# Two weight matrices kept in DRAM unsplit, one load fewer at the start, attention in pairs: a change to an attention-and-two-MLP kernel

## Chip, core and metric

The kernel runs on one core of a Trainium2 chip. The metric is the device time of one execution in microseconds (us), as a median over executions; lower is better.

## What is computed

Eight heads of attention over 4 batches of 576 tokens, four heads with a local mask (a window of 32 keys) and four with a strided one (every 32nd key); then two multilayer blocks over the 2304 tokens:

```
attn = softmax(mask(q k^T / 8)) v              # B=4, H=8, S=576, D=64
x    = attn as (2304, 512)
x    = (((x @ w1) * (x @ w2)) @ w3) @ w_out     # 512 -> 1024 -> 1024 -> 512
h    = x @ w_in                                 # 512 -> 2048
out  = (h * sigmoid(1.702 h)) @ w_out2          # 2048 -> 512
```

The weights arrive as 8-byte floats.

## The kernel before

Every matmul operand is held as two parts, hi and lo, whose sum is the fp32 value, and every product is three matmuls (hi·lo, lo·hi, hi·hi). Making the two parts is a **split**: `split_hi` (L171) is a copy on ACT, `split_lo` (L177) a subtraction on DVE. A weight piece of 8-byte floats (1 MB, 128 x 1024 values) is turned to fp32 by `to_f32`: L192 and L193 on ACT, L194, L195 and L196 on DVE.

The program runs in these stages (times from the profiled execution):

- **Start, 0 to 36 us.** Attention of batch 0, in 11 parts (`a_load`, `a_scores`, `a_trans`, `a_pv`), beside the first pieces of w1 and w2 (`c_load` fetches, `c_do` converts).
- **First layer of batches 0 and 1, 36 to 198 us.** `g1` (matmuls L354) makes (x w1)(x w2). The attention of the next batches and the conversion of the other pieces are woven in. Half of the results go to DRAM (`abdram`) and come back later.
- **Fold, 198 to 236 us.** `w_group` (L468) multiplies w3 by w_out once, so that the first block's second half is one product.
- **Back region, 236 to 316 us.** `g2` (matmuls L400, copy `ysb` L406, write to `ydram` L408) for batches 0 and 1; the results parked in `abdram` are read back and split (`back`, L389, tile `ab`). Attention parts of batch 2, and units 0 to 3 of w_in, are woven in.
- **Batch 2, 316 to 405 us, and batch 3, 405 to 487 us.** `g1` and `g2` of these; the other units of w_in in batch 2; the eight units of the second w_out (units 8 to 15) in batch 3.
- **Second block, 487 us to the end.** For each of 3 token blocks of 768 and each of 8 units: `quad` (7 products of 6 matmuls, L657, by a Strassen-like scheme, adds L663, gelu L648) and `o_group` (L703).

A **unit** is handled by `u_load` (fetch, L526) and `u_conv`. A w_in unit is converted into tile `x`, four sums or differences are added to it, the seven 256-wide factors are split into tile `hl` (128 x 1792 twice) and written to `widram` (L544). A w_out unit is converted into `x`, split back into its own `raw` tile and written to `wodram` (L551). In the second block `w_load` reads `hl` straight from `widram` (L614) and `wt_load` reads a w_out unit straight into its slot (L637); all eight `wt_load` are issued ahead of the first quad. `x` is one buffer; `raw` is two.

The order of instructions on each engine is fixed before the run by a scheduler, from the order in which `weave` emits the steps of several lists; each engine runs its list in order. All DMAs are issued by SP, in its order, on one queue.

Of the kernel before, what the change touches and what calls it, by code (L numbers as in the profile page):

```python
# [11 lines left out]
F32 = mybir.dt.float32  # L12
F32R = mybir.dt.float32r
# [3 lines left out]
I64 = mybir.dt.int64  # L17
# [4 lines left out]
P = 128  # L22
B, H, S, D = 4, 8, 576, 64
# [4 lines left out]
STRIDE = 32  # L28
# [109 lines left out]
def body(ctx: ExitStack, tc, qk, vv, mask, w1, w2, w3t, wo, win, wout, out):  # L138
# [21 lines left out]

    ydram = dram.tile([KC, P, NT], F32, name="ydram")
    abdram = dram.tile([3, MC, P, HB], F32, name="abdram")
    widram = dram.tile([NU, P, 2, 7 * 256], F32, name="widram")
    wodram = dram.tile([NU, P, 2, CW2], F32, name="wodram")

    def r(ap):
        return ap.bitcast(F32)

    def split_hi(hi, src, eng="act"):
        if eng == "act":  # L170
            nc.scalar.activation(hi, src, AF.Copy)  # L171
# [52 lines left out]
    def a_load(n):  # L224
        if n >= n_all or n in raws:
            return
        tl = ALL[n]
        nk, w = tl.nk, 2 * (tl.nq + tl.nk)
        t = at.tile([P, ATW], F32, tag="qk", name="qk", bufs=3)
        nc.sync.dma_start(t[:, :w], qk[n, :, :w])  # L230
        u = at.tile([P, HL * D], F32, tag="v", name="v", bufs=4)
        nc.sync.dma_start(u[:nk], vv[n, :nk])
        raws[n] = (t, u)

    def a_scores(n):
        tl = ALL[n]
        nq, nk = tl.nq, tl.nk
        t, u = raws.pop(n)
        L = live[n] = dict(v=u)
        mi = MASKS.index(tl.mask)  # L240
        qs = t[:, :2 * nq].rearrange("p (h n) -> p h n", h=2)
        ks = t[:, 2 * nq:2 * (nq + nk)].rearrange("p (h n) -> p h n", h=2)
        sm = at.tile([P, HL, P], F32, tag="sm", name="sm", bufs=3)
        st = at.tile([P, 3, HL], F32, tag="st", name="st", bufs=3)

        sc = aps.tile([P, 2, 4 * P], F32, tag="sc", name="sc")
        for i in range(2):
            for g in range(2):
                rows = slice(g * D, (g + 1) * D)
                nc.tensor.matmul(  # L250
                    sc[:nq, g, i * P:i * P + nk], qs[rows, i], ks[rows, i], start=True, stop=True,
                )

        for h in range(HL):
            nc.vector.tensor_tensor_reduce(  # L255
                sm[:nq, h, :nk], sc[:nq, h // 2, h % 2 * P:h % 2 * P + nk], msk[:nq, mi, :nk], -SCALE, 3e38,
                op0=ALU.add, op1=ALU.min, accum_out=st[:nq, 0, h:h + 1],
            )
        for h in range(HL):
            nc.scalar.activation(  # L260
                sm[:nq, h, :nk], sm[:nq, h, :nk], AF.Exp, bias=st[:nq, 0, h:h + 1], scale=-1.0,
                accum_out=st[:nq, 1, h:h + 1],
            )
        nc.vector.tensor_scalar_add(st[:nq, 2], st[:nq, 1], EPS)
        nc.vector.reciprocal(st[:nq, 2], st[:nq, 2])
        nc.vector.tensor_tensor(
            sm[:nq, :, :nk], sm[:nq, :, :nk], st[:nq, 2].unsqueeze(2).to_broadcast([nq, HL, nk]), op=ALU.mult
        )
        L["sm"] = sm

# [20 lines left out]
    def a_pv(n):
        tl = ALL[n]
        nq, nk = tl.nq, tl.nk
        L = live.pop(n)
        ps = L["ps"]
        pv = aps.tile([P, 2, P], F32, tag="pv", name="pv")
        xh, xl = xt[tl.b]
        if tl.local:
            dh, dl = (x[:, 0:2, tl.o:tl.o + nq] for x in (xh, xl))
        else:  # L300
            dh, dl = (
                x[:, 2:4].rearrange("p c (j r) -> p c j r", r=STRIDE)[:, :, tl.j0:tl.j0 + tl.nj, tl.o:tl.o + tl.g]
                for x in (xh, xl)
            )

        for h in range(HL):
            rows = slice(h % 2 * D, (h % 2 + 1) * D)
            nc.tensor.matmul(  # L308
                pv[rows, h // 2, :nq], L["v"][:nk, h * D:(h + 1) * D], ps[:nk, h * nq:(h + 1) * nq],
                start=True, stop=True,  # L310
            )
        src = pv[:, :, :nq]
        if not tl.local:
            src = src.rearrange("p c (j r) -> p c j r", j=tl.nj)
        split_hi(dh, src)
        split_lo(dl, src, dh)

    def steps_for(b):

        out = []  # L320
        per = len(PARTS[b])
        for j in range(per):
            n = START[b] + j
            out.append((j + AT[0], lambda n=n: a_scores(n)))
            out.append((j + AT[1], lambda n=n: a_load(n + 2)))
            out.append((j + AT[2], lambda n=n: a_trans(n)))
            out.append((j + AT[3], lambda n=n: a_pv(n)))
        return sorted(((at / (per + AT[3] - 1), f) for at, f in out), key=lambda t: t[0])
# [120 lines left out]
    def c_load(i):  # L449
        if i < len(line):  # L450
            fetched[i] = fetch(line[i][1])

    def c_do(i):
        convert(line[i][0], fetched.pop(i))
        c_load(i + 3 if i + 3 < 20 else i + 2)

    def conv(*which):
        return [lambda i=i: c_do(i) for i in which]
# [26 lines left out]
    a_load(0)  # L485
    nc.sync.dma_start(msk, mask)
    a_load(1)
    for i in range(3):
        c_load(i)
    weave(steps_for(0), list(zip((0.1, 0.5), conv(0, 1))))  # L490

# [2 lines left out]
    def pairs(b, aways):  # L494
        return [f for m in range(MC) for hb in range(2) for f in g1(b, hb, m, hold, aways[hb])]

    places = (0.02, 0.1, 0.22, 0.34, 0.46, 0.58)
    weave(pairs(0, (None, 0)), steps_for(1), list(zip(places, conv(2, 3, 4, 5, 6, 7))))
    later = share(steps_for(2), 0.3, 0.25, 0.2, 0.25)
# [21 lines left out]
    def u_load(i):  # L521

        if i >= 2 * NU:
            return
        raw = cv[i % len(cv)].tile([P, CW2], I64, tag="raw", name="raw", bufs=2 if len(cv) == 1 else 1)
        nc.sync.dma_start(raw, win[i] if i < NU else wout[i - NU])  # L526
        todo[i] = raw

    def u_conv(i, last=False):
        raw = todo.pop(i)  # L530
        x = cv[0].tile([P, 2 * CW2], F32, tag="x", name="x")
        if i < NU:
            hl = cv[0].tile([P, 2, 7 * 256], F32R, tag="hl", name="hl")
            to_f32(x[:, :CW2], raw, CW2)
            if not last:
                u_load(i + 2)
            a21, a11, a12, a22, s1, s2, s3, s4 = (x[:, n * 256:(n + 1) * 256] for n in range(8))
            nc.vector.tensor_tensor(s1, a21, a22, op=ALU.add)
            nc.vector.tensor_tensor(s2, s1, a11, op=ALU.subtract)
            nc.vector.tensor_tensor(s3, a11, a21, op=ALU.subtract)  # L540
            nc.vector.tensor_tensor(s4, a12, s2, op=ALU.subtract)
            split_hi(hl[:, 0], x[:, 256:])
            split_lo(hl[:, 1], x[:, 256:], hl[:, 0])
            nc.sync.dma_start(widram[i], r(hl))  # L544
        else:

            to_f32(x[:, :CW2], raw, CW2)
            hl = raw.bitcast(F32R).rearrange("p (a n) -> p a n", a=2)
            split_hi(hl[:, 0], x[:, :CW2])
            split_lo(hl[:, 1], x[:, :CW2], hl[:, 0])  # L550
            nc.sync.dma_start(wodram[i - NU], r(hl))  # L551
            if not last:
                u_load(i + 2)

    def u_convs(lo, hi, ahead=True):
        return [lambda i=i: u_conv(i, not ahead and i + 2 >= hi) for i in range(lo, hi)]
# [54 lines left out]
    def w_load(n):  # L611
        if n < NB * NU:
            t = (p2 if n % 2 else cv_a).tile([P, 2, 7 * 256], F32R, tag="hl", name="hl")
            nc.sync.dma_start(r(t), widram[n % NU])  # L614
            wq[n] = t

    g = batch_groups(3)
# [16 lines left out]
    acc_l, acc_r = {}, {}  # L634

    def wt_load(i):
        nc.sync.dma_start(r(wt[i].rearrange("p a c n -> p a (c n)")), wodram[i])  # L637

    def g_split(src):
        t = ring[used[0] % len(ring)]  # L640
# [77 lines left out]

    wt_load(0)
    w_load(1)  # L720
    for i in range(1, NU):
        wt_load(i)
    for b in range(NB):
        left = [accp.tile([P, 512], F32, tag="acc", name="acc") for _ in range(HT // P)]
        for i in range(NU):
            quad(b, i, (lambda i=i: o_group(left, gl.pop(i - 1), i - 1, 0)) if i else (lambda: None))
            if i:
                o_group(left, gl.pop(NU + i - 1), i - 1, 1)
        for h in range(2):
# [45 lines left out]
```

## Time and profile before

| | |
|---|---|
| time, median of 3 (lowest to highest) | 873.87 us (873.4 to 874.31) |
| profiled execution: time, span of the core | 876.68 us, 874.9 us |
| mean granted TensorE clock | 0.982 |
| busy: PE, DVE, ACT | 830.2, 560.3, 418.3 us |
| moved by DMA | 151.77 MB |

The page of a profile has the busy time of each engine, and a chain of work that ended last. The trace behind it can be asked for the busy time of each engine in a stretch, for the waits of an engine and what ended each, and for single instructions with their start and duration. PE is TensorE, PEld its weight load, DVE VectorE, ACT ScalarE, SP the engine that issues the DMAs. A clock of 1.00 is full speed (2.4 GHz), 0.50 half.

### The profile page before, as it was taken

Reading aid. Unit: us, or ns where it says so; the run is one execution under the profiler, and the core shown is the slowest. Engines: PE = TensorE matmul, PEld = TensorE weight load, DVE = VectorE, ACT = ScalarE, POOL = GpSimd, SP = SyncE. Lnnn points to the kernel's source line nnn. Section 1 sums busy time; section 2 is a strip of 40 time slices with the busy share of each in tenths; the row PEclk is TensorE's granted clock in tenths of the full one; section 3 lists DMA queues with packets and bytes.
Section 4 is the critical chain, followed back from the end, with each engine's and each line's share of the span. In section 5 each row is a group of like instructions: output and inputs, shape, how many; then the busy total and the mean of one; then the engine's idle time right before and its main releaser. Section 6 shows DMA issues by size and latency. Waiting matters only on the chain.

```text
span 874.9 us, 13887 instructions
## 1 busy us (share of the span) xinstructions
PE 830.2 (95%) x5200; PEld 753.2 (86%) x5200; DVE 560.3 (64%) x1352; ACT 418.3 (48%) x980; POOL 1.4 (0%) x8
## 2 busy tenths in 40 slices
PE   3889999999998899999999599999999999999998
PEld 2679999987787899999999489998999988999986
DVE  6889983358888778755666356666455655655640
ACT  7888872246666556554455323344223433322330
POOL 0000000000000000000000000000000000000000
PEclk9999999999998899999999699999999999999999
DMA  8565561134477875415479964452344451344201
GB/s 294 175 228 177 165 200 58 63 120 134 139 281 254 283 272 235 159 35 203 175 273 349 349 267 169 169 190 88 112 176 152 148 194 37 136 161 161 85 36 37
DMA packets 41699, 151.77 MB, mean 173 GB/s; under 512 B 4512, under 2 KB 25888, under 8 KB 31904
## 3 DMA queue, kind: packets, MB, share of 16 engines
q1 hardware_dynamic: 41632, 150.88, 48.0%
q8 instruction: 41, 0.67, 0.3%
q14 instruction: 26, 0.21, 0.1%
HBM read 114.82 MB, written 36.04 MB: 172 GB/s over the span
## 4 chain that ended last, share of the span: by engine, by line
PE 84%; DVE 6%; ACT 5%; DMA 3%; issue 1%; SPq 0%; ACTq 0%; DVEq 0%
PE ps L354 23%; PE acc L703 23%; PE ps L657 20%; PE ps L400 10%; PE pv L308 2%; PE acc L468 2%; PE sc L250 2%; PE pt L286 1%; ACT sm L260 1%; DMA raw<-in_w3t 1%; DMA wodram<-raw 1%; DMA raw<-in_w 1%; DMA ydram<-ysb 1%; DVE xw L195 1%; DVE w L177 1%
## 5 line engine op out<-in xcount | busy, mean ns | idle before, releaser
L703 PE MATMUL acc<-w,w 128*128 128x512 f32 x864 | 204.4, 391 | 0.4 <-DVE w L177 0.4
L657 PE MATMUL ps<-yq,hl 128*128 128x384 f32 x1008 | 186.6, 341 | 10.5 <-ACT c L675 10.3
L657 PEld LDWEIGHTS ps<-yq,hl 128*128 128x128 f32 x1008 | 180.1, 190 | 14.6 <-ACT c L675 10.6
L703 PEld LDWEIGHTS acc<-w,w 128*128 128x128 f32 x864 | 161.6, 188 | 32.6 <-DVE w L177 1.2
L400 PE MATMUL ps<-ab,w 128*128 128x288 f32 x768 | 113.2, 309 | 5.8 <-DVE ab L177 2.9
L400 PEld LDWEIGHTS ps<-ab,w 128*128 128x128 f32 x768 | 109.1, 200 | 8.2 <-DVE ab L177 3.6
L354 PE MATMUL ps<-xbh,w 128*128 128x288 f32 x512 | 106.0, 300 | 0.0
L354 PE MATMUL ps<-xah,w 128*128 128x288 f32 x512 | 102.0, 295 | 0.0
L354 PEld LDWEIGHTS ps<-xbh,w 128*128 128x128 f32 x512 | 83.9, 191 | 0.8 <-issue 0.7
L354 PEld LDWEIGHTS ps<-xah,w 128*128 128x128 f32 x512 | 82.0, 188 | 0.0
L648 ACT ACTIVATE sg<-c 128x384 f32<-128x384 f32 x48 | 25.2, 525 | 115.0 <-DVE c L663 115.0
L354 PE MATMUL ps<-xbl,w 128*128 128x288 f32 x256 | 80.1, 313 | 0.0
L354 PE MATMUL ps<-xal,w 128*128 128x288 f32 x256 | 76.3, 298 | 0.0
L260 ACT ACTIVATE sm<-sm,st 96x128 f32<-96x128 f32 (+2 forms) x176 | 67.6, 387 | 13.9 <-DVE st L255 13.7
L663 DVE TENSOR_TENSOR u<-ps,u 128x384 f32<-128x384 f32 x96 | 53.3, 555 | 20.6 <-PE ps L657 19.8
L379 DVE TENSOR_TENSOR abf<-ps,abf 128x288 f32<-128x288 f32 x64 | 29.0, 453 | 40.7 <-PE ps L354 36.8
L354 PEld LDWEIGHTS ps<-xbl,w 128*128 128x128 f32 x256 | 49.1, 192 | 3.0 <-issue 0.2
L177 DVE TENSOR_TENSOR w<-gr,w 128x384 fp32r<-128x384 f32 x48 | 26.6, 558 | 38.4 <-ACT w L171 38.4
L255 DVE CUSTOM_DVE_ANT_0 sm<-sc,msk 96x128 f32<-96x128 f32 (+2 forms) x176 | 41.2, 276 | 14.2 <-PE sc L250 8.5
L468 PE MATMUL acc<-w,w 128*128 128x512 f32 x192 | 48.1, 402 | 1.2 <-ACT raw L476 0.8
L354 PEld LDWEIGHTS ps<-xal,w 128*128 128x128 f32 x256 | 48.1, 188 | 0.9 <-issue 0.2
L377 ACT ACTIVATE abf<-ps 128x288 f32<-128x288 f32 x64 | 25.8, 404 | 44.5 <-PE ps L354 44.3
(81 smaller groups left out, 1012.1 us busy)
## 6 DMA issues: line engine op xcount, KB each, us to landing
hl<-widram SPq DMA_DIRECT2D x24, 1792.0 KB
widram<-hl SPq DMA_DIRECT2D x8, 1792.0 KB
raw<-in_w3t SPq DMA_DIRECT2D x17, 512.0 KB
raw<-in_w SPq DMA_DIRECT2D x8, 1024.0 KB
raw<-in_win SPq DMA_DIRECT2D x8, 1024.0 KB
raw<-in_wout SPq DMA_DIRECT2D x8, 1024.0 KB
wodram<-raw SPq DMA_DIRECT2D x8, 1024.0 KB
w<-wodram SPq DMA_DIRECT2D x8, 1024.0 KB
```

What stands on the lines that cost most here:

```text
L177: e.tensor_tensor(lo, src, r(hi), op=ALU.subtract)
L255: nc.vector.tensor_tensor_reduce(sm[:nq, h, :nk], sc[:nq, h // 2, h % 2 * P:h % 2 * P + nk], msk[:nq, mi, :nk], -SCALE, 3e38, op0=ALU.add, ...
L260: nc.scalar.activation(sm[:nq, h, :nk], sm[:nq, h, :nk], AF.Exp, bias=st[:nq, 0, h:h + 1], scale=-1.0, accum_out=st[:nq, 1, h:h + 1],)
L354: nc.tensor.matmul(ps, ws[a][m // 2][:, at:at + P], xh[c][:, k, cols], start=(k == 0 and (a, c) == ORDER[0]), stop=(k == KC - 1 and (a, c) ...
L377: nc.scalar.activation(f, ps, AF.Copy)
L379: nc.vector.tensor_tensor(f, ps, f, op=ALU.mult)
L400: nc.tensor.matmul(st[0], wfs[a][k][:, n * P:(n + 1) * P], hold[hb, k][:, c], start=(k == 0 and (a, c) == ORDER[0]), stop=(k == MC - 1 and ...
L468: nc.tensor.matmul(acc[f], hl[:, a, f * P:(f + 1) * P], wor[c][g], start=(g == 0 and (a, c) == ORDER[0]), stop=(g == MC - 1 and (a, c) == ...
L648: nc.scalar.activation(sg, src, AF.Sigmoid, scale=1.702)
L657: nc.tensor.matmul(ps, w[:, a, f * 256 + kk * P:f * 256 + (kk + 1) * P], yq[:, b, kk, c], start=(kk == 0 and (a, c) == ORDER[0]), stop=(kk ...
L663: nc.vector.tensor_tensor(dst, x, y, op=ALU.add)
L703: nc.tensor.matmul(acc[t], g[:, a, t * P:(t + 1) * P], wt[i][:, c, half], start=(i == half == 0 and (a, c) == ORDER[0]), stop=(i == NU - 1 ...
```

## The change

Three edits:

- **Weights unsplit in DRAM.** `widram` and `wodram` hold one fp32 value where they held a hi and a lo. `u_conv` splits nothing any more and writes `x` itself (after: L562 and L564); so `x` is held until its write has landed. `w_load` reads 896 KB into `x` and splits it into `hl`, 24 times; `wt_load` reads 512 KB into `raw` and splits it into the slot, 8 times, and is issued one unit ahead of its use, not all eight at first. `u_conv` now fetches the unit after next ahead of its own write for w_out too.
- **Start.** Two weight pieces are fetched at first, not three; pieces 2 to 4 are fetched after the attention of batch 0 has been emitted.
- **Pairs.** For batches 1 to 3 two attention parts share one `a_scores` (one PSUM tile `sc`), and one `a_pv`; `qk` has 4 buffers, not 3.

```
-    widram = dram.tile([NU, P, 2, 7 * 256], F32, name="widram")
-    wodram = dram.tile([NU, P, 2, CW2], F32, name="wodram")
+    widram = dram.tile([NU, P, 7 * 256], F32, name="widram")
+    wodram = dram.tile([NU, P, CW2], F32, name="wodram")
...
+        if b:
+            for j in range(0, per, 2):
+                n = START[b] + j
+                ns = [n, n + 1][:per - j]
+                out.append((j + AT[0], lambda ns=ns: a_scores(*ns)))
+                out.append((j + 1.0, lambda n=n: a_load(n + 2)))
+                out.append((j + 1.4, lambda n=n: a_load(n + 3)))
+                out.append((j + 1.8, lambda ns=ns: [a_trans(n) for n in ns]))
+                out.append((j + 2.6, lambda ns=ns: a_pv(*ns)))
...
-        c_load(i + 3 if i + 3 < 20 else i + 2)
+        if i > 1:
+            c_load(i + 3 if i + 3 < 20 else i + 2)
...
-    for i in range(3):
+    for i in range(2):
         c_load(i)
...
+    for i in range(2, 5):
+        c_load(i)
...
         x = cv[0].tile([P, 2 * CW2], F32, tag="x", name="x")
+        to_f32(x[:, :CW2], raw, CW2)
+        if not last:
+            u_load(i + 2)
         if i < NU:
-            hl = cv[0].tile([P, 2, 7 * 256], F32R, tag="hl", name="hl")
-            to_f32(x[:, :CW2], raw, CW2)
-            if not last:
-                u_load(i + 2)
...
-            split_hi(hl[:, 0], x[:, 256:])
-            split_lo(hl[:, 1], x[:, 256:], hl[:, 0])
-            nc.sync.dma_start(widram[i], r(hl))
+            nc.sync.dma_start(widram[i], x[:, 256:])
         else:
-            to_f32(x[:, :CW2], raw, CW2)
-            hl = raw.bitcast(F32R).rearrange("p (a n) -> p a n", a=2)
-            split_hi(hl[:, 0], x[:, :CW2])
-            split_lo(hl[:, 1], x[:, :CW2], hl[:, 0])
-            nc.sync.dma_start(wodram[i - NU], r(hl))
-            if not last:
-                u_load(i + 2)
+            nc.sync.dma_start(wodram[i - NU], x[:, :CW2])
...
             t = (p2 if n % 2 else cv_a).tile([P, 2, 7 * 256], F32R, tag="hl", name="hl")
-            nc.sync.dma_start(r(t), widram[n % NU])
+            x = cv_a.tile([P, 2 * CW2], F32, tag="x", name="x")[:, 256:]
+            nc.sync.dma_start(x, widram[n % NU])
+            split_hi(t[:, 0], x)
+            split_lo(t[:, 1], x, t[:, 0])
...
     def wt_load(i):
-        nc.sync.dma_start(r(wt[i].rearrange("p a c n -> p a (c n)")), wodram[i])
+        t = cv_a.tile([P, CW2], I64, tag="raw", name="raw").bitcast(F32)[:, :CW2]
+        nc.sync.dma_start(t, wodram[i])
+        w = wt[i].rearrange("p a c n -> p a (c n)")
+        split_hi(w[:, 0], t)
+        split_lo(w[:, 1], t, w[:, 0])
...
-    for i in range(1, NU):
-        wt_load(i)
     for b in range(NB):
...
+            if b == 0 and i + 1 < NU:
+                wt_load(i + 1)
```

What this moves on the engines shows best in three places. The first is ACT at the start of the back region, before: the conversions of units 0 to 2 (`raw`, `x`), the split `hl` of unit 0, copies `ysb` and splits `ab`.

```order
L406 ACTIVATE ysb_2704<-ps_2654 128x288
L192 ACTIVATE x_2801<-raw_2646 128x1024
L193 ACTIVATE raw_2646<-raw_2646 128x1024
L406 ACTIVATE ysb_2742<-ps_2713 128x288
L193 ACTIVATE raw_2648<-raw_2648 128x1024
L171 ACTIVATE hl_2802<-x_2801 128x1792
L406 ACTIVATE ysb_2770<-ps_2745 128x288
L171 ACTIVATE ab_2819<-abf_2817 128x288
L171 ACTIVATE ab_2824<-abf_2822 128x288
L171 ACTIVATE ab_2829<-abf_2827 128x288
L406 ACTIVATE ysb_2798<-ps_2773 128x288
L193 ACTIVATE raw_2808<-raw_2808 128x1024
```

The same place after:

```order
L192 ACTIVATE x_2791<-raw_2654 128x1024
L193 ACTIVATE raw_2654<-raw_2654 128x1024
L424 ACTIVATE ysb_2691<-ps_2662 128x288
L193 ACTIVATE raw_2656<-raw_2656 128x1024
L424 ACTIVATE ysb_2732<-ps_2707 128x288
L424 ACTIVATE ysb_2760<-ps_2735 128x288
L171 ACTIVATE ab_2806<-abf_2804 128x288
L193 ACTIVATE raw_2797<-raw_2797 128x1024
L171 ACTIVATE ab_2811<-abf_2809 128x288
L171 ACTIVATE ab_2816<-abf_2814 128x288
L424 ACTIVATE ysb_2788<-ps_2763 128x288
L192 ACTIVATE x_3463<-raw_2656 128x1024
```

The 128 x 1792 split is gone from between the `ysb` copies, and the first conversion step of unit 2 (L193 on `raw_2797`), which waits for that unit's load, has moved from behind the last `ysb` of the group to between two splits of `ab`.

The second place is ACT at the end of batch 3, before: the last four `ysb` of the batch, units 14 (`x_5224`) and 15 (`x_5312`) of the weights, and the first copy `c` of the second block.

```order
L406 ACTIVATE ysb_5408<-ps_5383 128x288
L192 ACTIVATE x_5224<-raw_5089 128x1024
L193 ACTIVATE raw_5089<-raw_5089 128x1024
L406 ACTIVATE ysb_5436<-ps_5411 128x288
L171 ACTIVATE raw_5089<-x_5224 128x1024
L406 ACTIVATE ysb_5464<-ps_5439 128x288
L192 ACTIVATE x_5312<-raw_5160 128x1024
L193 ACTIVATE raw_5160<-raw_5160 128x1024
L406 ACTIVATE ysb_5492<-ps_5467 128x288
L171 ACTIVATE raw_5160<-x_5312 128x1024
L675 ACTIVATE c_5521<-ps_5514 128x384
```

After, the same four `ysb`; units 13, 14 and 15 are `x_5090`, `x_5161` and `x_5247`, with the raw tiles `raw_4962`, `raw_5027` and `raw_5096`:

```order
L424 ACTIVATE ysb_5341<-ps_5316 128x288
L424 ACTIVATE ysb_5369<-ps_5344 128x288
L424 ACTIVATE ysb_5397<-ps_5372 128x288
L193 ACTIVATE raw_5027<-raw_5027 128x1024
L192 ACTIVATE x_5090<-raw_4962 128x1024
L424 ACTIVATE ysb_5425<-ps_5400 128x288
L193 ACTIVATE raw_5096<-raw_5096 128x1024
L192 ACTIVATE x_5161<-raw_5027 128x1024
L192 ACTIVATE x_5247<-raw_5096 128x1024
L171 ACTIVATE w0_66<-raw_5434 128x1024
L693 ACTIVATE c_5457<-ps_5450 128x384
```

Unit 13 stands where unit 15 stood; units 14 and 15 and the split of the first w_out unit stand between the last `ysb` and `c`. L193 of a unit now stands ahead of L192 of the unit before it.

The third place is SP after, from the load of unit 15 (`raw_5096`) on:

```order
L547 DMA raw_5096<-in_wout 128x1024
L564 DMA wodram_87<-x_5090 128x1024
L564 DMA wodram_87<-x_5161 128x1024
L652 DMA raw_5434<-wodram_87 128x1024
L652 DMA raw_5446<-wodram_87 128x1024
L564 DMA wodram_87<-x_5247 128x1024
L626 DMA x_5439<-widram_86 128x1792
L652 DMA raw_5535<-wodram_87 128x1024
```

Before, the last write of a w_out unit was followed by direct reads into slots and `hl`; now the read of the second w_in unit (`x_5439`) needs the buffer `x` that the last write frees.

## Rows read from the trace of the kernel before

**Rows 1.** Page, busy time of PE, and shares of the chain that ended last.

```profile
PE 830.2 (95%) x5200; PEld 753.2 (86%) x5200; DVE 560.3 (64%) x1352; ACT 418.3 (48%) x980; POOL 1.4 (0%) x8
...
PE 84%; DVE 6%; ACT 5%; DMA 3%; issue 1%; SPq 0%; ACTq 0%; DVEq 0%
```

**Rows 2.** Stretches: from:to, length; busy PE, PEld, DVE, ACT, POOL; clock; DMA share; GB/s.

```profile
0.00:22.00 22.00, 8.63 (x56) 6.18 (x56) 13.49 (x42) 15.46 (x37) 1.42 (x8) 1.00 0.82 294
...
88.00:110.00 22.00, 21.98 (x190) 19.88 (x191) 21.17 (x60) 18.30 (x54) 0.00 (x0) 1.00 0.50 155
...
532.00:554.00 22.00, 22.00 (x116) 20.53 (x116) 12.86 (x26) 6.84 (x14) 0.00 (x0) 1.00 0.45 171
```

**Rows 3.** Chain of waits, start: start, us, what; then PE's waits, 0 to 66.

```profile
3.09 7.31 DMA raw<-in_w
...
PE sc L250 <- DMA qk<-in_qk: 6.1, 2, 3.2
```

**Rows 4.** The same stretches view, back region.

```profile
250.00:264.00 14.00, 11.83 (x91) 10.54 (x91) 12.82 (x43) 8.37 (x27) 0.00 (x0) 0.89 0.79 271
264.00:280.00 16.00, 12.50 (x97) 11.21 (x97) 13.20 (x38) 11.54 (x26) 0.00 (x0) 0.93 0.73 274
280.00:300.00 20.00, 19.53 (x145) 18.90 (x145) 13.93 (x39) 9.40 (x23) 0.00 (x0) 0.88 0.79 270
300.00:316.00 16.00, 13.85 (x89) 13.12 (x86) 13.32 (x43) 10.87 (x37) 0.00 (x0) 0.79 0.72 256
```

**Rows 5.** PE's waits, 198 to 310: total, times, longest.

```profile
PE ps L400 <- ACT ysb L406: 2.9, 1, 2.9
PE ps L400 <- DVE ab L177: 2.4, 2, 2.1
PE sc L250 <- DVE st L255: 2.1, 2, 1.9
```

**Rows 6.** Chain of waits, back region, three of 99 pieces.

```profile
278.28 0.40 ACT ysb L406
...
298.34 1.70 ACT hl L171
...
302.01 0.46 DVE ab L177
```

**Rows 7.** Groups by line and form: count, busy, mean ns of one, idle before.

```profile
L193 ACT ACTIVATE raw<-raw 128x1024 int32<-128x1024 uint32 x28 | 32.3, 1152 | 2.5 <-DMA raw<-in_win 1.8 <-DMA raw<-in_wo 0.7
...
L177 DVE TENSOR_TENSOR hl<-x,hl 128x1792 fp32r<-128x1792 f32 x8 | 16.2, 2024 | 5.9 <-ACT hl L171 5.9
...
L171 ACT ACTIVATE hl<-x 128x1792 fp32r<-128x1792 f32 x8 | 13.6, 1699 | 5.0 <-DVE x L541 5.0
...
L177 DVE TENSOR_TENSOR raw<-x,raw 128x1024 fp32r<-128x1024 f32 x8 | 9.8, 1223 | 5.8 <-ACT raw L171 4.7 <-DMA ydram<-ysb 1.1
```

**Rows 8.** SP and ACT, single instructions: a load, units 8, 14 and 15.

```profile
415.74 0.33 SPq L526 DMA_DIRECT2D raw<-in_wout  x1
...
420.71 1.14 ACT L192 ACTIVATE x<-raw 128x1024 f32<-128x1024 f32 x1 [0.29 <-DMA raw<-in_wout]
...
473.49 1.13 ACT L192 ACTIVATE x<-raw 128x1024 f32<-128x1024 f32 x1
...
482.54 1.13 ACT L192 ACTIVATE x<-raw 128x1024 f32<-128x1024 f32 x1 [2.65 <-DMA raw<-in_wout]
```

**Rows 9.** Chain of waits, end of batch 3, four of 33 pieces.

```profile
476.75 1.22 DVE x L196
...
485.97 2.18 DMA ydram<-ysb
...
489.39 7.54 DMA wodram<-raw
...
497.58 6.00 PE ps L657 x18
```

**Rows 10.** PE, single runs: the second quad's start.

```profile
506.87 5.46 PE L657 MATMUL ps<-yq,hl 128*128 128x384 f32 x30
```

More of the change, by code (lines that the diff above doesn't have):

```diff
@@ L228, in a_load @@
         nk, w = tl.nk, 2 * (tl.nq + tl.nk)
-        t = at.tile([P, ATW], F32, tag="qk", name="qk", bufs=3)
+        t = at.tile([P, ATW], F32, tag="qk", name="qk", bufs=4)
         nc.sync.dma_start(t[:, :w], qk[n, :, :w])
@@ L233, in a_load, with a_scores, a_soft @@
         raws[n] = (t, u)
-    def a_scores(n):
+    def a_scores(*ns):
+        sc = aps.tile([P, 2, 4 * P], F32, tag="sc", name="sc")
+        for at_c, n in zip((0, 2 * P), ns):
+            nq, nk = ALL[n].nq, ALL[n].nk
+            t, u = raws.pop(n)
+            live[n] = dict(v=u)
+            qs = t[:, :2 * nq].rearrange("p (h n) -> p h n", h=2)
+            ks = t[:, 2 * nq:2 * (nq + nk)].rearrange("p (h n) -> p h n", h=2)
+            for i in range(2):
+                for g in range(2):
+                    rows = slice(g * D, (g + 1) * D)
+                    c0 = at_c + i * P
+                    nc.tensor.matmul(sc[:nq, g, c0:c0 + nk], qs[rows, i], ks[rows, i], start=True, stop=True)
+        for at_c, n in zip((0, 2 * P), ns):
+            a_soft(n, sc[:, :, at_c:at_c + 2 * P])
+    def a_soft(n, sc):
         tl = ALL[n]
         nq, nk = tl.nq, tl.nk
-        t, u = raws.pop(n)
-        L = live[n] = dict(v=u)
+        L = live[n]
         mi = MASKS.index(tl.mask)
-        qs = t[:, :2 * nq].rearrange("p (h n) -> p h n", h=2)
-        ks = t[:, 2 * nq:2 * (nq + nk)].rearrange("p (h n) -> p h n", h=2)
         sm = at.tile([P, HL, P], F32, tag="sm", name="sm", bufs=3)
         st = at.tile([P, 3, HL], F32, tag="st", name="st", bufs=3)
[L246 to L252, printed above, removed]
         for h in range(HL):
@@ L289, in a_trans, with a_pv @@
         L["ps"] = ps
[L291 to L316, printed above, removed]
+    def a_pv(*ns):
+        pvs = aps.tile([P, 4, P], F32, tag="pv", name="pv")
+        for j, n in enumerate(ns):
+            nq, nk = ALL[n].nq, ALL[n].nk
+            L = live.pop(n)
+            ps = L["ps"]
+            for h in range(HL):
+                rows = slice(h % 2 * D, (h % 2 + 1) * D)
+                nc.tensor.matmul(
+                    pvs[rows, 2 * j + h // 2, :nq], L["v"][:nk, h * D:(h + 1) * D], ps[:nk, h * nq:(h + 1) * nq],
+                    start=True, stop=True,
+                )
+        for j, n in enumerate(ns):
+            tl = ALL[n]
+            xh, xl = xt[tl.b]
+            src = pvs[:, 2 * j:2 * j + 2, :tl.nq]
+            if tl.local:
+                dh, dl = (x[:, 0:2, tl.o:tl.o + tl.nq] for x in (xh, xl))
+            else:
+                dh, dl = (
+                    x[:, 2:4].rearrange("p c (j r) -> p c j r", r=STRIDE)[
+                        :, :, tl.j0:tl.j0 + tl.nj, tl.o:tl.o + tl.g
+                    ] for x in (xh, xl)
+                )
+                src = src.rearrange("p c (j r) -> p c j r", j=tl.nj)
+            split_hi(dh, src)
+            split_lo(dl, src, dh)
     def steps_for(b):
@@ L321, in steps_for @@
         per = len(PARTS[b])
+        if b:
[7 more added lines that the diff above has]
+                out.append((j + 2.6, lambda ns=ns: a_pv(*ns)))
+            return sorted(((at / (per + 1.7), f) for at, f in out), key=lambda t: t[0])
         for j in range(per):
@@ L487, in body @@
     a_load(1)
-    for i in range(3):
+    for i in range(2):
         c_load(i)
```

## The prediction, made before the changed kernel ran

> **What bounds the kernel now.** I read the page first: TensorE (PE) is busy for 830.2 of 874.9 us and holds 84% of the chain that ended last [rows 1]. A change that leaves the matmuls as they are, as this one does, can only move PE's idle time, 45 us, and the time at half clock behind it. So the second view is the table of stretches, to see where that idle time lies [rows 2]. In 0 to 22 us PE works for 8.63 us. In the first layer it is full, with DVE at 21.17 of 22 us, so DVE has no slack there. In the second block it is full with DVE at 12.86 and ACT at 6.84 of 22 us, so both have room. Two other holes are left: the back region [rows 4] and the boundary between batch 3 and the second block [rows 9]. The waits and the chain of these two, read third, carry the forecast.
>
> **Start and pairs: about -1 us.** Three pieces of 1 MB are queued at 3.09 us; the first lands 7.31 us later [rows 3]. The attention loads that follow stand behind all three, and PE waits 6.1 us for `qk` in two waits. With two pieces one such transfer leaves the way of those loads. But ACT is busy for 15.46 us of the first 22 [rows 2], so part of the wait comes back as a wait for ACT or DVE. I take a third of it, -2 us; bounds -5 (nearly the whole wait goes) and +1 (the third piece is now late). The conversion deferred falls into a stretch where PE is full and DVE nearly so: +1 (0 to +2). The pairs change no arithmetic. They halve the handshakes on `sc` and `pv` and make each part's result later. No row here shows a paired part; the nearest is the wait `sc` <- `st`, 2.1 us [rows 5], which halved gives -1 and doubled +2; I count it inside the back region's range.
>
> **Back region: about -9 us.** From 250 to 316 us PE is idle for 2.17 + 3.50 + 0.47 + 2.15 = 8.3 us, and the clock costs (1 - 0.89) x 14 + (1 - 0.93) x 16 + (1 - 0.88) x 20 + (1 - 0.79) x 16 = 8.4 us more [rows 4]: 16.7 us lost. What ends the waits are `ysb` on ACT and `ab` on DVE [rows 5]. Both stand behind the split of `hl` [rows 6]: one `ysb` starts at 278.28, behind a 1.70 us copy; the copy at 298.34 and its 2.02 us subtraction [rows 7] end just ahead of the `ab` at 302.01 on which PE starts again. The change takes four pairs of these out of the region (4 x 1.70 on ACT, 4 x 2.02 on DVE) and halves four writes of 1.79 MB, behind which the reads of `abdram` wait. If all of it went, the gain would be 16.7 us. But something is late next: in the new order L193 of unit 2 stands between two `ab` splits, and waits for a load of 1 MB that lands 4.97 us after its issue (415.74 to 420.71) [rows 8]. I allow 2.8 us of idle time for this (the load less what of it lies beside queued matmuls) and 1.6 us for the attention waits, which are 2.1 us now [rows 5], 4.4 in all, and as much clock loss for each idle microsecond as now (8.4 / 8.3): 16.7 - 8.8 = 8, and 1 us for the shorter writes: -9. Bounds -13 (the new wait is hidden too) and -3 (another wait of the same size in each place of the old).
>
> **Batch 2: +0.5 us.** L192 of each unit now waits until the write of `x` has landed. The eight w_in units share 236 to 405 us, some 20 us each, against a write of about 5 us (the line of the next part), so the write is over; bounds 0 and +1.5.
>
> **Boundary: about +13 us.** Before, unit 8 starts L192 at 420.71 and unit 15 at 482.54 [rows 8]: 8.83 us a unit. The last write, 7.54 us from 489.39, releases `c` and with it PE at 497.58 [rows 9]; the second quad starts at 506.87 [rows 10]. After, `x` is held until its write has landed, and on ACT, which runs its list in order, L193 of unit i+2 stands ahead of L192 of unit i+1, so that this waits for the load of unit i+2. The loop of one unit is then: L192 start to L196 end, 473.49 to 477.97 = 4.5 us [rows 8, 9]; the raw buffer is free, load of unit i+2, 5.0 us; L193, 1.15 us [rows 7]: 10.6 us, and with some of ACT's other work in it 11.2. Unit 8 itself starts later, at about 427, since the first `w_load` is now split ahead of it (1.7 + 2.0 us, behind a transfer and the batch's own copies).
>
> - Unit 14 starts at 427 + 6 x 11.2 = 494.2 and is done at 498.7.
> - Its write, 512 KB, lies between the 144 KB write of 2.18 us [rows 9] and the 1 MB load of 4.97 us: on the line between them 3.3 us. Unit 15 waits for it: 502.0.
> - Unit 15 takes 4.5 us and, with the first w_out split between its steps (1.2 us), is done at 507.7. PE starts again at about 508, not 497.58.
> - The second quad needs its `w_load`: write of unit 15, 3.3 us; read of 896 KB, by the same line 4.6 us; the split 1.7 + 2.0 us, and 0.5 us of issue: 519.8, against 506.87: +13.
>
> What PE does in the meantime, the first quad and its `o_group`, is done in both cases. Bounds: the pace of the unit is the uncertain factor; at 10.4 us a unit +8, at 11.9 us +17. [...]
>
> **Second block: +0.5 us.** 24 splits of 1.70 us on ACT and 2.02 us on DVE, and 8 smaller ones, are added. A quad with its share of `o_group` takes some 15 us of PE; DVE goes from 58% to about 72%, ACT from 31% to about 42%. PE waits for neither now, so four PSUM buffers hide it. The single `x` lets one read and split of about 8.3 us (4.6 + 1.7 + 2.0) stand in each such period. Bounds 0 and +3.
>
> **Sum.** -2 + 1 - 9 + 0.5 + 13 + 0.5 = +4 us, on the profiled execution's 876.68 us. The median is 2.8 us below that, so 873.87 + 4 = 878 us.
>
> **Rivals.**
>
> - *The boundary's chain doesn't run out (faster).* If the loads are prefetched early enough the units keep the pace of 8.83 us. Then unit 15 starts at 427 + 61.8 = 488.8, is done at 494.5, PE starts at 495, and the second quad at 494.5 + 3.3 + 4.6 + 4.2 = 506.6: no loss, and the sum is -9: 865 us. For it: of the units shown only the last waits long for its load, 2.65 us [rows 8], and the bytes are halved. Against it: the one buffer and the order on ACT. It decides whether unit 13 starts L192 before 475 us (471 by this, 483 by mine).
> - *The back region keeps its holes (slower, by more).* The splits go, but `ab` and `ysb` wait behind L193 or L192, which wait for loads. For it: queue share 0.72 to 0.79 there [rows 4]. Against it: the rows name the split, not a load. The term is -3, the sum +10: 884 us.
> - *The splits in the second block reach PE.* If the split's DVE half comes late in each period and the next `w_load` with it, a wait of 0.8 us for each of 23 quads gives +18: 892 us or more. Against it: the room in rows 2.
>
> **How the numbers follow.** About 0.2%, 1.75 us, is what a measurement of this kernel can tell from no change. Mine has 0.47 (its own range 872 to 884: slower 0.30, same 0.13, faster 0.04), the boundary without loss 0.24 (faster 0.22, same 0.02), the kept holes 0.19 (slower 0.18, same 0.01), the splits on PE 0.06 (slower), and 0.04 for what I did not think of, spread evenly. That is faster 0.28, same 0.17, slower 0.55. The range takes in the middle of the first rival and most of the second: 864 to 887.
>
> **What would show it.** In the profile after: L171 and L177 of 128 x 1792 only in the second block; PE idle and clock loss from 250 to 316 us about half of now; L192 of w_out units 11 us apart, waiting for the DMA of `wodram`; the second quad about 13 us later after the start of batch 3; DVE near 72% in the second block with PE full. It would be wrong if the last `ysb` of batch 3 were delayed so that PE stops earlier still, or if unit 15 were done before PE is.

## The result, and the profile after

The changed kernel takes 881.46 us (median of 4, 879.37 to 882.67) against 873.63 us; the ratio is 1.0091, 95% interval 1.0073 to 1.0108. It is slower by 7.8 us, where +4 was forecast. A second set of runs gave 1.0074 (1.0050 to 1.0098).

PE does the same matmuls, is busy less and idle longer, as the first rows of the page say (against [rows 1]; 877.6 - 818.5 = 59 us idle, 45 before):

```profile
PE 818.5 (93%) x5200; PEld 746.2 (85%) x5200; DVE 585.1 (67%) x1368; ACT 437.4 (50%) x996; POOL 1.4 (0%) x8
...
PE 67%; DMA 12%; ACT 9%; DVE 9%; issue 2%; SPq 1%; ACTq 0%; DVEq 0%
```

DMA's share of the chain has gone from 3% to 12%, though 114 MB are moved where 152 MB were. To see where the time went, each stage is taken from the first matmul of its kind to the first of the next stage (first layer, fold, `g2`, batch 2, batch 3, first quad, second quad); by this measure the fold begins at 183 us before. In us, with one profiled execution of each kernel; "start", "pairs" and "unsplit" are one edit alone, and they and the last two columns are the experiments below:

| stage | before | after | after, 2nd | start | pairs | unsplit | two x | start + pairs |
|---|---|---|---|---|---|---|---|---|
| start | 35.8 | 31.9 | 31.7 | 30.3 | 35.2 | 34.6 | 31.5 | 31.6 |
| first layer | 147.3 | 145.1 | 145.5 | 148.6 | 147.1 | 148.7 | 145.9 | 145.9 |
| fold | 53.0 | 53.8 | 53.4 | 53.7 | 53.4 | 53.5 | 53.7 | 52.9 |
| back region | 79.0 | 63.2 | 63.5 | 78.6 | 69.0 | 61.6 | 62.4 | 70.3 |
| batch 2 | 90.3 | 97.0 | 97.4 | 90.3 | 86.9 | 98.3 | 91.4 | 86.9 |
| batch 3 | 77.0 | 83.1 | 85.8 | 77.0 | 77.7 | 78.8 | 85.7 | 77.0 |
| to the second quad | 24.5 | 33.1 | 33.3 | 21.5 | 21.2 | 41.2 | 11.7 | 19.3 |
| rest | 368.0 | 370.3 | 370.1 | 368.1 | 368.0 | 370.3 | 371.5 | 368.0 |
| span | 874.9 | 877.6 | 880.8 | 868.1 | 858.6 | 886.9 | 853.8 | 852.0 |

So the changed kernel won 15.8 us in the back region and 5.3 us before it (3.9 and 2.2, less 0.8 in the fold), and gave 6.7 us back in batch 2, 6.1 in batch 3, 8.7 at the boundary and 2.3 in the second block. In these two executions that is +2.7 us, where the medians say +7.8.

A stage also gets shorter when work leaves it. The back region and batch 2, before and after, as whole stretches:

```profile
236.06:315.08 79.02, 70.74 (x520) 66.26 (x518) 61.60 (x180) 49.00 (x129) 0.00 (x0) 0.89 0.76 270
315.08:405.42 90.34, 90.34 (x729) 85.36 (x727) 62.00 (x177) 45.92 (x121) 0.00 (x0) 1.00 0.49 183
230.79:293.96 63.17, 58.99 (x468) 55.74 (x466) 38.68 (x105) 32.37 (x80) 0.00 (x0) 1.00 0.69 234
293.96:391.00 97.04, 92.06 (x757) 88.61 (x757) 66.65 (x234) 47.37 (x156) 0.00 (x0) 0.96 0.35 125
```

After the change 52 matmuls fewer fall into the back region (468, not 520) and 28 more into batch 2: attention parts that the new order puts elsewhere. Of the 15.8 us, PE's idle time is 4.1 (8.3 before, 4.2 after) and its busy time 11.7; the busy part holds both the clock and the moved matmuls, which are worth some 3 us by an estimate from the trace (sixteen `sc` took 1.06 us at full clock).

The stretches of the after kernel (columns as in [rows 2]), which answer to [rows 2, 4]; the rows from 231 to 294 us are its back region:

```profile
0.00:22.00 22.00, 11.61 (x76) 8.16 (x76) 13.47 (x53) 14.87 (x43) 1.42 (x8) 1.00 0.82 281
231.00:245.00 14.00, 13.80 (x105) 13.57 (x104) 7.27 (x13) 7.50 (x12) 0.00 (x0) 1.00 0.64 238
245.00:259.00 14.00, 12.52 (x104) 11.32 (x103) 11.02 (x41) 7.52 (x26) 0.00 (x0) 1.00 0.70 217
259.00:273.00 14.00, 12.06 (x102) 11.20 (x101) 8.66 (x26) 8.25 (x23) 0.00 (x0) 1.00 0.67 219
273.00:294.00 21.00, 20.43 (x163) 19.49 (x161) 11.52 (x27) 9.03 (x18) 0.00 (x0) 1.00 0.72 251
308.00:330.00 22.00, 20.12 (x175) 18.95 (x173) 15.13 (x61) 12.05 (x40) 0.00 (x0) 1.00 0.64 229
330.00:352.00 22.00, 18.91 (x146) 18.34 (x147) 16.58 (x53) 10.27 (x37) 0.00 (x0) 0.84 0.27 95
462.00:484.00 22.00, 15.85 (x99) 15.53 (x99) 6.10 (x7) 4.79 (x7) 0.00 (x0) 0.84 0.54 170
484.00:506.00 22.00, 7.15 (x27) 6.25 (x28) 15.07 (x21) 9.75 (x13) 0.00 (x0) 0.62 0.46 160
```

In the back region PE is idle for 4.2 us and the clock stays at 1.00 throughout. In batch 2 (328 to 333 us) and between 458 and 498 us there are new holes, and each has a clock below 1.00 in the row in which it ends. In the second block PE is full, with DVE at 230 of 344 us (189 before):

```profile
532.00:876.00 344.00, 339.14 (x1684) 305.29 (x1683) 188.72 (x353) 113.54 (x218) 0.00 (x0) 1.00 0.34 126
532.00:876.00 344.00, 341.63 (x1694) 306.58 (x1692) 229.67 (x377) 143.41 (x241) 0.00 (x0) 1.00 0.23 79
```

The first row is before, the second after. PE's waits (total, times, longest), the first line before, the others after, against [rows 3, 5]:

```profile
PE ps L657 <- ACT c L675: 10.3, 1, 10.3
PE ps L675 <- ACT c L693: 19.0, 1, 19.0
PE ps L418 <- DVE ab L177: 13.6, 6, 5.0
PE sc L249 <- DMA qk<-in_qk: 3.3, 1, 3.3
PE sc L249 <- DVE st L262: 2.3, 3, 1.5
```

The chain of waits in batch 2 shows where one of the `ab` waits, 5.0 us, comes from:

```profile
321.68 5.43 DMA raw<-in_win
...
327.13 1.13 ACT raw L193
328.26 1.54 ACT sm L267 x8
...
332.69 0.36 DVE ab L177
...
333.09 7.18 PE ps L418 x39
```

ACT stood at L193 of a w_in unit until its load had landed (3.0 us of idle time); the exponentials of an attention part and the split `ab` were behind it in ACT's list, and PE behind these.

At the boundary, L192 and L193 of the w_out units on ACT (in brackets the idle time before and what ended it), which answer to [rows 8]; then the chain of waits, against [rows 9], and PE:

```profile
410.72 1.14 ACT L192 ACTIVATE x<-raw 128x1024 f32<-128x1024 f32 x1 [1.46 <-DVE hl L177]
...
446.42 1.12 ACT L193 ACTIVATE raw<-raw 128x1024 int32<-128x1024 uint32 x1 [4.67 <-DMA raw<-in_wout]
...
482.85 1.10 ACT L193 ACTIVATE raw<-raw 128x1024 int32<-128x1024 uint32 x1 [8.04 <-DMA raw<-in_wout]
484.05 1.12 ACT L192 ACTIVATE x<-raw 128x1024 f32<-128x1024 f32 x1
491.39 1.12 ACT L192 ACTIVATE x<-raw 128x1024 f32<-128x1024 f32 x1 [6.23 <-DMA wodram<-x]
```

```profile
440.30 6.09 DMA raw<-in_wout
...
453.36 7.00 DMA wodram<-x
...
477.35 6.67 DMA wodram<-x
...
484.05 1.13 ACT x L192
...
487.19 1.24 DVE x L196
...
488.44 2.87 DMA wodram<-x
...
491.39 1.12 ACT x L192
```

```profile
497.47 4.97 PE L675 MATMUL ps<-yq,hl 128*128 128x384 f32 x18 [18.97 <-ACT c L693]
503.82 3.63 PE L721 MATMUL acc<-w,w 128*128 128x512 f32 x14 [1.38 <-ACT w L171]
507.29 0.87 PE L675 MATMUL ps<-yq,hl 128*128 128x384 f32 x4
```

Unit 14 starts at 484.05, 73.3 us after unit 8: 12.2 us a unit, where it was 8.83. Unit 15 waits for the write of unit 14, and `c` for unit 15; PE stands for 19 us. SP issues the load of a later unit just ahead of the write that frees `x`:

```profile
452.98 0.33 SPq L547 DMA_DIRECT2D raw<-in_wout  x1
453.36 0.42 SPq L564 DMA_DIRECT2D wodram<-x  x1
```

That write landed after 7.00 us and the one at 477.35, also behind a load, after 6.67; the last one, with no load ahead of it, after 2.87. So a conversion of 4.4 us (484.05 to 488.43) and a write of some 7 us behind a load make up most of the 12.2 us; the load itself takes 6.09 us in the chain.

### The profile page after: what moved, and what is told of

Same layout as the page of the kernel before. It is cut to its first block, busy times and chain, and to the rows that moved or that the text cites. A ratio compares the mean times of both kernels' runs of the same rounds, so it can differ in the third digit from the quotient of the medians.

```text
span 877.6 us, 13922 instructions
## 1 busy us (share of the span) xinstructions
PE 818.5 (93%) x5200; PEld 746.2 (85%) x5200; DVE 585.1 (67%) x1368; ACT 437.4 (50%) x996; POOL 1.4 (0%) x8
## 4 chain that ended last, share of the span: by engine, by line
PE 67%; DMA 12%; ACT 9%; DVE 9%; issue 2%; SPq 1%; ACTq 0%; DVEq 0%
PE acc L721 22%; PE ps L675 19%; PE ps L372 13%; PE ps L418 7%; DMA wodram<-x 4%; ACT sm L267 2%; PE sc L249 2%; DMA widram<-x 2%; PE pv L306 2%; DMA raw<-in_w3t 1%; ACT xw L192 1%; ACT x L192 1%; PE pt L293 1%; DMA ydram<-ysb 1%; DVE w L177 1%
## 5 line engine op out<-in xcount | busy, mean ns | idle before, releaser
L675 PE MATMUL ps<-yq,hl 128*128 128x384 f32 x1008 | 185.9, 339 | 20.2 <-ACT c L693 19.0
L675 PEld LDWEIGHTS ps<-yq,hl 128*128 128x128 f32 x1008 | 179.2, 189 | 24.6 <-ACT c L693 19.3
L418 PE MATMUL ps<-ab,w 128*128 128x288 f32 x768 | 109.8, 302 | 13.6 <-DVE ab L177 13.6
L418 PEld LDWEIGHTS ps<-ab,w 128*128 128x128 f32 x768 | 105.5, 193 | 16.4 <-DVE ab L177 15.0
L267 ACT ACTIVATE sm<-sm,st 96x128 f32<-96x128 f32 (+2 forms) x176 | 67.3, 385 | 11.9 <-DVE st L262 11.2
L193 ACT ACTIVATE raw<-raw 128x1024 int32<-128x1024 uint32 (+1 forms) x44 | 42.6, 970 | 38.7 <-DMA raw<-in_wout 22.3
L177 DVE TENSOR_TENSOR hl<-x,hl 128x1792 fp32r<-128x1792 f32 x24 | 48.6, 2024 | 16.9 <-ACT hl L171 16.7
L262 DVE CUSTOM_DVE_ANT_0 sm<-sc,msk 96x128 f32<-96x128 f32 (+2 forms) x176 | 39.2, 275 | 21.3 <-PE sc L249 16.1
```

Of the source, the lines that this page charges most:

```text
L193: nc.scalar.activation(ri[:, :, 0], ru[:, :, 0], AF.Copy, scale=LOW)
L262: nc.vector.tensor_tensor_reduce(sm[:nq, h, :nk], sc[:nq, h // 2, h % 2 * P:h % 2 * P + nk], msk[:nq, mi, :nk], -SCALE, 3e38, op0=ALU.add, ...
L267: nc.scalar.activation(sm[:nq, h, :nk], sm[:nq, h, :nk], AF.Exp, bias=st[:nq, 0, h:h + 1], scale=-1.0, accum_out=st[:nq, 1, h:h + 1],)
L418: nc.tensor.matmul(st[0], wfs[a][k][:, n * P:(n + 1) * P], hold[hb, k][:, c], start=(k == 0 and (a, c) == ORDER[0]), stop=(k == MC - 1 and ...
L675: nc.tensor.matmul(ps, w[:, a, f * 256 + kk * P:f * 256 + (kk + 1) * P], yq[:, b, kk, c], start=(kk == 0 and (a, c) == ORDER[0]), stop=(kk ...
```

## The experiments

The theory after the result: (a) the loss is the one buffer `x`, held until a write has landed, which puts a load, a conversion and a write in a row; (b) the gains come from the start and from the back region. The rivals: the late loads themselves, the reads through `x` in the second block, and the pairs as the source of the back region's gain.

**Each edit alone.** The start alone:

```
-    for i in range(3):
+    for i in range(2):
         c_load(i)
...
+    for i in range(2, 5):
+        c_load(i)
```

> The kernel before with the edit of the start alone (two pieces fetched at first, pieces 2 to 4 after batch 0). Theory: the first layer starts 3.9 us earlier in the changed kernel because the attention loads of batch 0 no longer stand behind a third transfer of 1 MB; this edit alone gives -3 to -5 us, about 870. Rival: the earlier start is given back when the late pieces are converted in the first layer, where DVE is full, and what stays of it in the changed kernel comes from the pairs; then it is within 1 us of 873.9.

Measured: 869.04 us, ratio 0.9943 (0.9923 to 0.9964), -4.9 us. The stage "start" is 5.4 us shorter and the first layer 1.3 us longer; the theory held in its size. PE's waits up to 66 us in this kernel:

```profile
PE sc L250 <- DMA qk<-in_qk: 3.4, 1, 3.4
PE pt L286 <- DVE sm L266: 2.6, 6, 0.5
```

The wait for the attention loads is 2.7 us shorter (6.1 before), the wait for `sm` 2.3 us (4.9 before), so not all of the gain is the loads' own. Of the first layer's 1.3 us, 1.0 are busy time of PE: that they are the price of the late piece isn't shown.

The pairs alone (`a_scores(*ns)`, `a_pv(*ns)`, the steps for batches 1 to 3, `qk` with 4 buffers):

> The kernel before with the pairs alone (and the fourth qk buffer). Theory: the pairs matter little by themselves, -1 to -3 us, since the holes of the back region are ended by the split of hl, which stays. Rival: the pairs took the attention's waits out of the back region and are half or more of its 15.8 us: -6 us or better, 868 or less. If pairing makes results late it is slower, +2.

Measured: 859.91 us, ratio 0.9838 (0.9812 to 0.9864), -14 us. The theory fell, the rival held: 10.0 us of it are in the back region, with all splits of `hl` still there, and 3.4 in batch 2 (the 3.3 at the boundary are the long execution of before, see the last run). The stretches of the back region of this kernel:

```profile
235.00:252.00 17.00, 16.65 (x125) 16.07 (x123) 10.09 (x15) 10.35 (x16) 0.00 (x0) 1.00 0.69 242
252.00:269.00 17.00, 16.51 (x143) 14.65 (x141) 13.78 (x46) 10.53 (x31) 0.00 (x0) 1.00 0.88 291
269.00:286.00 17.00, 13.63 (x109) 12.68 (x108) 12.72 (x36) 9.29 (x25) 0.00 (x0) 1.00 0.73 247
286.00:305.00 19.00, 18.01 (x143) 16.06 (x142) 18.31 (x64) 14.48 (x49) 0.00 (x0) 1.00 0.88 311
```

PE is still idle for 5.2 us, 3.1 less than before, one wait of it 2.4 us long:

```profile
PE ps L418 <- ACT ysb L424: 3.3, 2, 2.4
```

But the clock is 1.00 in every row, where it was 0.79 to 0.93 [rows 4]. PE's busy time in the stage falls by 6.9 us (70.7 to 63.8). The prediction had put the cost of the clock there at 8.4 us; the larger part of the gain is this busy time, though 12 attention matmuls have left the stage here too.

Whether the fourth buffer does it was asked next:

```
-        t = at.tile([P, ATW], F32, tag="qk", name="qk", bufs=3)
+        t = at.tile([P, ATW], F32, tag="qk", name="qk", bufs=4)
```

> The kernel before with the fourth qk buffer alone (no pairs). Theory: pairing itself, which halves the alternations between the two engines on sc and pv, makes the holes of the back region shorter so that the clock doesn't fall; the buffer alone gives less than 2 us, 872 or more. Rival: the earlier attention loads are what helps; then most of the 14 us of the pairs are here, 863 or less.

Measured: 872.86 us, ratio 0.9990 (0.9968 to 1.0012). No change that can be told: the buffer alone is not what helps. What in the pairing does it, the fewer alternations or the other order of instructions that comes with it, and whether it needs the fourth buffer, is not separated.

The unsplit weights alone:

> The kernel before with the unsplit weights alone. Theory: it carries the back region's gain (-11 to -15) and all of the losses, batch 2 +6.7, batch 3 and boundary +14.8, ramp of the second block +2.3; sum +9 to +13, 883 to 887. Rival: the back region's gain needs the pairs too; then the unsplit weights alone gain less than 8 there and cost +16 or more, 890.

Measured: 885.35 us, ratio 1.0144 (1.0121 to 1.0166), +12 us. The theory held in the sum, with both terms larger than it said: the back region is 17.4 us shorter here too, without the pairs, though some 38 of its attention matmuls have gone to batch 2. So the two edits win the same holes, and the gain is made once: -10.0 and -17.4 alone, -15.8 together. The losses are all this edit's: batch 2 +7.9, batch 3 and boundary +18.5, rest +2.3.

**Which part of the unsplit weights.** First w_out as before, all else changed. With the lines shown, `u_load` stands behind the write again for w_out, and all eight `wt_load` read straight into their slots ahead of the first quad:

```
+            hl = raw.bitcast(F32R).rearrange("p (a n) -> p a n", a=2)
+            split_hi(hl[:, 0], x[:, :CW2])
+            split_lo(hl[:, 1], x[:, :CW2], hl[:, 0])
+            nc.sync.dma_start(wodram[i - NU], r(hl))
-            nc.sync.dma_start(wodram[i - NU], x[:, :CW2])
```

> The changed kernel with the second w_out split before its write as in the kernel before (w_in stays unsplit, start and pairs stay). Theory: the loop load, convert, write of the w_out units with one x buffer is what costs batch 3 and the boundary; without it 12 to 15 us come back, 867 to 870, faster than both. Rival: the loss is the one x buffer through which w_in units come back (read, split) and the late second unit; then only the wait on the w_out write goes and 4 us or less come back, 877.

Measured: 870.4 us, ratio to before 0.9968 (0.9945 to 0.9991); 11 us came back, of the 12 to 15 expected. Batch 2 stays at 97.5 us, and from batch 3 to the end this kernel takes 477.6 us, before 469.5 and after 486.6: 8 us of loss are left (11 or so if the boundary of before is taken at its usual 21 us). Two rows of ACT, the split of the first w_in unit that came back and L192 of unit 8:

```profile
406.55 1.70 ACT L171 ACTIVATE hl<-x 128x1792 fp32r<-128x1792 f32 x1 [0.59 <-DMA x<-widram]
410.35 1.13 ACT L192 ACTIVATE x<-raw 128x1024 f32<-128x1024 f32 x1 [1.46 <-DVE hl L177]
```

Unit 8 needs `x`, which holds the w_in unit until both halves of its split are made; it starts 20.2 us into batch 3 (which begins at 390.1), 14.0 us in the kernel with start and pairs alone. Unit 15 starts 86.7 us in, against 74.8, and `c` follows it. So the read that comes back through the one `x` has a part: 6.2 of these 11.9 us. The other 5.7 are a slower pace from unit 8 to unit 15; ACT waits longer for loads in it, and why was not tested.

Then the buffer itself: all edits kept, two tiles `x` for w_in, and the two halves of one tile for w_out (a w_out unit fills only half of `x`):

```
+        if i < NU:
+            x = cv[0].tile([P, 2 * CW2], F32, tag="x", name="x", bufs=2)
+        else:
+            if i == NU:
+                halves[0] = cv[0].tile([P, 2 * CW2], F32, tag="x", name="x")
+            x = halves[0][:, i % 2 * CW2:(i % 2 + 1) * CW2]
-        x = cv[0].tile([P, 2 * CW2], F32, tag="x", name="x")
```

> The changed kernel with two buffers for x in the conversions: two tiles for the w_in units, the two halves of one tile for the w_out units. Theory: one buffer makes L192 of a unit wait for the write of the unit before and puts L193 of the unit after it ahead, which waits for a load; with two, batch 2 loses its stall (-6.7 us), batch 3 its stall (-6) and the boundary's chain shortens (-4 to -8): 862 to 867. Rival: the loads themselves are late (queue), whatever the buffers; then batch 2 stays within 2 us of 97 and the time within 3 us of 881.

Measured: 854.77 us, ratio to before 0.9774 (0.9752 to 0.9795): 27 us faster than the changed kernel, more than expected. Batch 2 falls from 97.0 to 91.4 (PE is idle there for 0.6 us, where it was 5.0, and the clock is 1.00), the boundary from 33.1 to 11.7. Batch 3 doesn't gain (85.7): there the theory failed, and the rival has its place. ACT's waits in batch 3 and PE's runs at the boundary of this kernel:

```profile
ACT raw L193 <- DMA raw<-in_wout: 15.5, 7, 5.0
```

```profile
470.57 4.33 PE L681 MATMUL ps<-yq,hl 128*128 128x384 f32 x24
477.25 9.43 PE L681 MATMUL ps<-yq,hl 128*128 128x384 f32 x42 [2.35 <-ACT c L699]
```

ACT still stands in front of loads for 15.5 us (22.3 in the changed kernel), and what is behind it there is late; but the last unit is done before PE reaches the boundary, and the wait for `c` is 2.35 us, not 19. Unit 15 starts at 450.16 us here, 45.4 us after unit 8: 6.5 us a unit. The load is still issued ahead of the write, so the second buffer alone undoes the loss at the boundary. Not tried is the other way out, one buffer with the write issued ahead of the load.

**Which to keep.** The two gains without the unsplit weights:

> The start and the pairs together, weights split before their write as in the kernel before. Theory: the two gains lie in different stages and add: -4.9 and -14 give 854 to 857, the best version. Rival: both shorten the same wait for attention loads, then it is no better than the pairs alone, 860.

Measured: 853.12 us, ratio 0.9757 (0.9734 to 0.9780). They add, and this is 2.4% faster than the kernel before and 3.2% faster than the changed one; the kernel with two buffers can't be told from it, as the intervals overlap.

Two mixtures, first w_in unsplit with two tiles `x` and w_out as before:

> Start, pairs, w_in unsplit with two x tiles, w_out split before its write as in the kernel before. Theory: the unsplit w_in gains some 7 us more than the pairs in the back region, and with two x tiles batch 2 no longer gives it back, while the later second w_in unit costs 6 to 9 us at the start of the second block: 856 to 864, no better than start and pairs. Rival: batch 2 keeps its stall of 6 to 7 us with two tiles: 868 to 871.

Measured: 865.75 us, ratio 0.9902 (0.9881 to 0.9922). Batch 2 is at 91.4 us, with PE idle for 0.6, so two tiles take its stall here too; what stays above the 86.9 of start and pairs goes with 40 more attention matmuls in the stage. The back region is the shortest of all, 61.2. But the first w_in unit that comes back stands ahead of unit 8 here too, and from the first quad on it loses 12 us to the kernel before and 17 to start and pairs (boundary 29.1, rest 375.5), where 6 to 9 were expected: slower than expected.

And w_out unsplit with two halves, w_in as before:

> Start, pairs, the second w_out unsplit with two halves of one x tile; w_in split before its write as in the kernel before. Theory: what each edit does lies in a stage of its own, so this has the back region and batch 2 of start and pairs (70.3 and 86.9 us), and batch 3 and the boundary of the run with two x tiles (85.7 and 11.7, in sum 1 us above start and pairs): 851 to 855, no gain over start and pairs. Rival: without the w_in reads and splits on the queue and on ACT, batch 3 loses its new waits for the loads too, and the sum is 844 to 848.

Measured: 853.17 us, ratio 0.9759 (0.9735 to 0.9783). Batch 2 is at 86.9 and the boundary at 12.8, but batch 3, at 81.7, and the second block, at 372.2, give 4.7 and 4.2 us back: the theory, no gain over start and pairs, though not by the stages that it named. The back region is 66.3 us here and 70.3 with start and pairs, with the same order of instructions on PE, ACT and DVE: so much can a stage of one execution differ without a difference in its instructions.

**The changed kernel again.**

> The changed kernel unaltered, for a second profile beside the runs of the kernel before on one chip. Theory: the profiled pair understated the loss (+2.7 us against +7.8 in the medians) because the profiled execution of before was a long one, 3 us of it in the boundary (24.5 us, against 21.0 to 21.5 with the same code there in three experiments); this profile then shows batch 2 near 97, batch 3 near 83 and the boundary at 33 or a little more. Rival: the changed kernel's own stages vary by 3 to 5 us from one execution to the next.

Measured: 880.37 us, ratio 1.0074 (1.0050 to 1.0098); the column "after, 2nd" of the table. The boundary of the profiled execution of before (24.5 us) was the long one, as the theory has it; but batch 3 of the changed kernel also differs by 2.7 us between its two profiles, so the rival has a part. The boundary is held against 21.0 to 21.5 us as well as 24.5 below.

## Why the prediction came out as it did

The direction and the main loss were right: +4 was forecast, +7.8 measured. That the sum came so near is luck, because its terms were wrong in both directions: forecast and profiled, start -1 and -5.3 (with first layer and fold), back region -9 and -15.8, batch 2 +0.5 and +6.7, batch 3 with the boundary +13 and +14.8, second block +0.5 and +2.3.

- **Boundary, +13: right in mechanism, too small in size.** Batch 3 and boundary cost 6.1 + 8.7 = 14.8 us in the first profile, and 8.8 + 8.9 = 17.7 in the second, to which some 3 us come if the usual 21 us of before are taken: then 18 to 21 us, above the bound of +17. Unit 8 started 19.7 us into batch 3 (21.6 forecast), the pace was 12.2 us a unit (11.2 taken, 11.9 the bound), the last write 2.87 us (3.3). The pace was short by the load and the write that run together: 6.09 us for the load, where 5.0 were taken, and 7.00 for the write behind it, where the loop had none. What was not seen is that ACT's waits in front of these loads, 22.3 us in six, also hold up batch 3's own work: PE's `ab` wait of 4.5 us at 458 us and the clock after it.
- **Back region, -9: mis-sized.** The stage is 15.8 us shorter, beyond the bound of -13, but some 3 us of that are attention matmuls that moved out of it, mostly to batch 2. The step that failed is "as much clock loss for each idle microsecond as now": PE is still idle for 4.2 us, near the 4.4 us allowed, and the clock cost is 0, not 4.4. That an idle microsecond costs clock at all in a fixed measure had no row behind it.
- **The pairs, nothing: mis-sized, by the most.** "They change no arithmetic" was true and beside the point; alone they give -14 us. No row showed a paired part, and the term rested on the wait `sc` <- `st` alone. In the sum the error hides, because the unsplit weights close the same holes.
- **Batch 2, +0.5: failed.** "The write is over" asked about L192 and its write alone. The order on ACT had put L193 of the next unit ahead of it; that waits for a load which SP can issue only when the conversion before has freed the raw buffer (SP waits 18.5 us for L196 there, in two waits). The prediction had this very step in the back region and at the boundary and didn't carry it to batch 2: PE is idle for 5.0 us there, and the stage is 6.7 us longer with the attention that moved into it.
- **Start, -1 with the late piece: mis-sized.** It is -4.9 alone. A third of the wait for `qk` was taken, and 2.7 of 6.1 us go; the step that failed is that part of it "comes back as a wait for ACT or DVE": the largest of these, for `sm`, is 2.3 us shorter too.
- **Second block, +0.5: the steady part right.** After 530 us PE waits 0.2 us in all, with DVE at 67% from 532 to 876 us (72% forecast) and ACT at 42% (42% forecast). Of the 2.3 us, 1.2 are a wait for the split of `hl` at 518 us; the wait of 1.4 us for the split of a w_out unit falls into the boundary.

The rival "the boundary's chain doesn't run out" was false for this kernel, and a second buffer makes it true: 854.77 us. The rival of the kept holes named the right wait, L193 in front of a load, but in the wrong stages: it opened holes of 5.0 us in batch 2 and 4.5 us in batch 3. The splits in the second block didn't reach PE; with that rival's +18 in place of +0.5 the forecast's own sum would have been some 895 us, not 892.

## What to carry to other kernels

A staging tile that is written to DRAM is held until the write has landed; where it was the only one, as here, load, conversion and write stood in a row, and on an engine that works in order everything behind the next conversion waited too. Before a hole is closed with a large edit, ask which small one closes it: here pairing the attention parts won 14 us alone, and the unsplit weights won the same holes a second time and paid for it elsewhere. When an idle hole also costs clock, price the two apart, since here the clock part vanished while half of the idle time stayed. And before a stage's gain is believed, count its instructions before and after.

## What was not expected of the hardware

The clock loss is not in proportion to the idle time: 8.3 us of idle time from 250 to 316 us stood beside 8.4 us of clock before, and with the pairs 5.2 us in the same stage cost none, though a single wait of 2.4 us remains. With start and pairs, a row of the same stage falls below 1.00 again, after a wait of 1.5 us:

```profile
262.00:280.00 18.00, 15.39 (x120) 14.08 (x119) 13.40 (x35) 9.60 (x25) 0.00 (x0) 0.91 0.70 235
```

What about the holes decides it is left open. The 512 KB write landed 2.87 us after the conversion when no load was queued ahead of it, and 6.67 and 7.00 us when it was queued behind a load of 1 MB.

The clock in the first rows is not to be taken at its word. The row from 0 to 22 us says 1.00, but eight matmuls of the same shape took 1.22 us there and 0.71 us later in the kernel before, so PE was at the lower of its two levels at first:

```profile
20.63 1.22 PE L250 MATMUL sc<-qk 64*126 64x126 f32 x8 [2.82 <-DMA qk<-in_qk]
60.36 0.71 PE L250 MATMUL sc<-qk 64*126 64x126 f32 x8
```
